# K loaded two groups to a transfer, its columns read in interleaved order, and wo's first 18 rows in one transfer

## The chip, the cores and the metric

The kernel runs on one core of a Trainium2 chip. The metric is the device time of one execution in microseconds (us). The kernel before took 100.55 us, the median of three runs (100.34 to 100.57).

The engines are named as in the profile: PE multiplies matrices (PEld loads its stationary operand), DVE and ACT work elementwise and reduce, POOL sets constants, and SP issues the DMA transfers. The engines run side by side and wait for each other on semaphores.

## The reference

The computation is one decoding step, for a single row x of 1024 values: attention with a sliding window beside a perceptron, both added to x.

```python
W = min(4096, max(256, Sk // 4))                  # 4096 of 65536 tokens
q = (xn @ wq).reshape(B, Sq, 32, 128)             # 32 query heads, xn = layernorm(x)
k = repeat(k_cache[:, :, Sk - W:, :], 8, axis=1)  # 4 groups of K and V, 8 heads each
v = repeat(v_cache[:, :, Sk - W:, :], 8, axis=1)
p = softmax(einsum("bhqd,bhkd->bhqk", q, k) * 128 ** -0.5)
A = einsum("bhqk,bhkd->bhqd", p, v).reshape(B, Sq, 4096) @ wo
Bm = gelu(layernorm(xn) @ w1 + b1) @ w2 + b2      # 1024 -> 3584 -> 1024
out = x + A + Bm
```

The parts that are read from the chip's memory, in bf16: K and V windows 4.19 MB each, wq 8.39 MB, wo 8.39 MB, w1 and w2 7.34 MB each. The profile counts 39.86 MB read.

## The kernel before

With one row of x each weight is used once. The row is the stationary operand and the weights stream through PE as the moving operand, 512 columns to a matmul. The transfers have an order written out by hand on SP's queue, and PE's program is in the same order:

1. SP issues K in four transfers (line 211), one for each of the four groups, then wq in two halves, then w1 in two halves.
2. DVE computes both layer norms, and then transposes K group by group into the tile KT (line 261), in blocks of 32 x 32. It waits for one K transfer before each of the four transposes.
3. When the last transpose is done, SP issues V into the tile KV that held K (line 264).
4. PE multiplies wq's rows (line 379, tile WA). The semaphore "q" releases SP to issue w2 into the same tile WA (line 269), and DVE to build the tile QBD of query columns.
5. PE multiplies the first half of w1 (`h_rows(0)`), then the scores (lines 409 to 414): 32 matmuls in two banks of 16, each with a stationary part of QBD and 512 columns of KT.
6. PE multiplies the second half of w1 (`h_rows(1)`) while DVE and ACT form the maximum, the exponentials and their transpose PT. The semaphore "h" releases SP to issue wo into the tile W1 (line 271).
7. PE forms the product of PT and V (line 454), then w2's rows (line 464) and then wo's rows (lines 479 to 492). wo's rows come in chunks of 10, 8, 6, 4, 2 and 1; a set of eight small transfers into the tile LOW, issued between the second and third chunk, holds the remaining row, split over two halves of the partitions. PE waits for each chunk's semaphore before its rows, and for ACT's two copies (line 357) before the last seven rows, whose results are packed differently (`tail_row`).
8. ACT and DVE copy the result, and SP stores it (line 365).

K's layout matters here. Before, partition p of KV holds, for each group, the 32 tokens 32p to 32p+31 with 128 values each. DVE's transpose exchanges partition and column inside each block of 32 x 32, so in KT the 32 tokens that lay in 32 partitions lie side by side. V stays in the layout that K had, and so the scores' columns have to come out in the order (i, q): i the token within a partition, q the partition within its block of 32.

W1 is read by `h_cols` (line 386) with four neighbouring columns at a time and a step of 28 columns (56 bytes). DVE has reductions whose input is read with a step: line 246 with 16 bytes, line 256 with 128 bytes, line 348 with 512 bytes. Line 297 reduces a contiguous row.

Of the kernel before, what the change touches and what calls it, by code (L numbers as in the profile page):

```python
# [9 lines left out]
D = 1024  # L10
F = 3584
HQ = 32
HKV = 4
DH = 128
REP = HQ // HKV
SK = 65536
W = 4096
# [3 lines left out]
W1_CHUNKS = [4, 4]  # L21
WQ_CHUNKS = [4, 4]
W2_CHUNKS = [16, 12]
WO_CHUNKS = [10, 8, 6, 4, 2, 1]
WO_HEAD = 4
WO_LOW = 18
XW = 136
QG = 520
# [22 lines left out]
def bass_parallel_sum__sliding_block_cached__mixer_channel_mlp__decode_kernel(  # L51
# [17 lines left out]
    pe, dve, act, pool, sp = nc.tensor, nc.vector, nc.scalar, nc.gpsimd, nc.sync  # L69

    def sems(name, n):
        return [nc.alloc_semaphore(f"{name}{i}") for i in range(n)]
# [2 lines left out]
    s_low = nc.alloc_semaphore("s_low")  # L75
    s_w1 = sems("s_w1", len(W1_CHUNKS))
    s_wq = sems("s_wq", len(WQ_CHUNKS))
    s_k = sems("s_k", HKV)
    s_wo = sems("s_wo", len(WO_CHUNKS))
    s_w2 = sems("s_w2", len(W2_CHUNKS))  # L80

# [6 lines left out]
    def sb(name, shape, d):  # L88
        return nc.alloc_sbuf_tensor(name, shape, d)
# [40 lines left out]
    KV = sb("KV", [128, 16384], bf16)  # L130
    KT = sb("KT", [128, 16384], bf16)
    W1 = sb("W1", [128, KC * F], bf16)
# [6 lines left out]
    def bank(n, rows=128, first=0):  # L139
        return PS[first:first + rows, n * 512:(n + 1) * 512]  # L140
# [4 lines left out]
    wo_p = A_wo.rearrange("(p j) n -> p j n", j=32)  # L145
# [4 lines left out]
    def load_chunks(dst, src, chunks, width, semaphores, c0=0):  # L150
        for j, n in enumerate(chunks):
            sp.dma_start(  # L152
                dst[:, c0 * width:(c0 + n) * width].rearrange("p (c n) -> p c n", c=n),
                src[:, c0:c0 + n, :],
            ).then_inc(semaphores[j], 16)
            c0 += n
# [51 lines left out]
    POOL.mark(pool.memset(PT[:, 1024:1024 + 96], 0.0))  # L208
    C["consts"] = POOL.cnt

    for g in range(HKV):
        sp.dma_start(  # L212
            KV[:, g * 4096:(g + 1) * 4096],
            A_k_cache[0, g, SK - W:SK, :].rearrange("(p i) d -> p (i d)", p=128)).then_inc(s_k[g], 16)
    load_chunks(WA, wq_p, WQ_CHUNKS, NQ, s_wq)
    load_chunks(W1, w1_p, W1_CHUNKS, F, s_w1)

# [39 lines left out]
        out=B32[:, :], in_=identf[:, :].rearrange("p (q r) -> p r q", q=4), axis=AX.X, op=ALU.add))  # L257

    for i in range(HKV):
        dve.wait_ge(s_k[i], 16)  # L260
        C["kt"] = DVE.mark(dve.transpose(KT[:, i * 4096:(i + 1) * 4096], KV[:, i * 4096:(i + 1) * 4096]))  # L261

    V = KV[:, :]
# [5 lines left out]
    sp.wait_ge(done["q"], 1)  # L269
    load_chunks(W2, w2_p, W2_CHUNKS, D, s_w2)  # L270
    sp.wait_ge(done["h"], 1)
    load_chunks(W1, wo_p, WO_CHUNKS[:2], D, s_wo)
    low_source = A_wo.rearrange("(u p j) n -> p u j n", u=2, j=32)[:, :, WO_MAIN, :]
    for first in (0, 1, 2, 3, 32, 33, 34, 35):
        sp.dma_start(  # L275
            LOW[first:first + 29:4, :].rearrange("p (u n) -> p u n", u=2),
            low_source[first:first + 29:4]).then_inc(s_low, 16)
    load_chunks(W1, wo_p, WO_CHUNKS[2:WO_HEAD], D, s_wo[2:], WO_LOW)
    load_chunks(WA, wo_p, WO_CHUNKS[WO_HEAD:], D, s_wo[WO_HEAD:], FC)

    dve.wait_ge(done["q"], 1)
# [123 lines left out]

    h_rows(0)
    pe.wait_ge(DVE.sem, C["d_QBD"])
    K5 = KT[:, :].rearrange("p (g i j k) -> p g i j k", g=HKV, i=32, j=4)
    for b in range(2):
        for n in range(16):  # L410
            g, j = n // 4, n % 4
            last = pe.matmul(bank(3 + b), lhsT=QBD[:, g * 512 + j * 128:g * 512 + j * 128 + 128],  # L412
                             rhs=K5[:, g, 16 * b:16 * b + 16, j, :], start=(n == 0), stop=(n == 15))
        last.then_inc(done["sc" if b else "sc0"], 1)
    def acc(a):
        return bank(7, 32, 32 * a)
# [35 lines left out]
    with pe.Fori(0, 4) as i:  # L452
        for u in range(8):
            pe.matmul(bank(1), lhsT=PT[:, bass.ds(i * 256 + u * 32, 128)], rhs=V4[:, :, bass.ds(i * 8 + u, 1), :],  # L454
                      start=False, stop=False, skip_group_check=True)
# [16 lines left out]
    for j in range(4):  # L472
        last = pe.matmul(PS[:, 2 * 512:2 * 512 + 32], lhsT=E4[:, j * 128:(j + 1) * 128],
                         rhs=ON[:, j * 32:(j + 1) * 32], start=(j == 0), stop=(j == 3))
# [3 lines left out]
    c0 = 0  # L478
    for j, n in enumerate(WO_CHUNKS):
        if c0 == WO_LOW:  # L480
# [6 lines left out]
        for c in range(c0, c0 + n):  # L487
            rhs = (W1 if c < FC else WA)[:, c * D:(c + 1) * D]
# [35 lines left out]
```

## Time and profile before

| What | Value |
|---|---|
| Median of three runs | 100.55 us |
| The profiled execution | 100.35 us |
| Its span, first to last instruction | 99.1 us |
| PE busy | 70.5 us (71%) |
| DVE busy | 37.5 us (38%) |
| DMA, mean over the span | 402 GB/s, 3286 packets |
| Scores (line 412), 32 matmuls | 7.1 us busy, first start 48.49 us |
| K transposes (line 261), 4 | 17.4 us busy, first start 17.18 us |
| K issues on SP | 0.80 to 3.00 us |

How to read it: the page cuts the span in 40 slices and gives the busy share of each in tenths. A group line names the line of the kernel, engine, operation, tiles and count, then busy time and mean ns of one, and then the idle time in front with what ended it. PE's matmuls overlap, so the distance between two starts, and not the duration of one, tells what a matmul costs in a stream. A timeline line begins with its start and its time in us. "DMA to landing" is the time from an issue to the last byte's arrival, and it includes the time in the queue.

### The profile page before, as it was taken

The numbers are of one execution on the slowest core, as the hardware profiler recorded it, in microseconds if no ns is written. First come the engines' busy times: TensorE is split into PE (matmuls) and PEld (weight loads), VectorE is DVE, ScalarE is ACT, GpSimd is POOL, SyncE is SP. The second block draws the span as 40 slices with busy tenths as digits, with TensorE's granted clock in tenths as the row PEclk, the third lists the DMA queues.
The fourth block names the chain that finished last, engine by engine and source line by source line (L and its number), as shares of the span: only waits on it lengthen the run. The fifth ranks groups of instructions, "written<-read, shape, count | busy, mean of one in ns | idle before, by whom it ended". The sixth has DMA issues, their size and how long they took to land.

```text
span 99.1 us, 1197 instructions
## 1 busy us (share of the span) xinstructions
PE 70.5 (71%) x341; PEld 28.4 (29%) x341; DVE 37.5 (38%) x56; ACT 5.7 (6%) x11; POOL 6.5 (7%) x26
## 2 busy tenths in 40 slices
PE   0021000305999999999999999799999999979532
PEld 0000000002334433334444344233335445422210
DVE  0007998999999900091002543440024010000001
ACT  0500004200000000000000040000000000000021
POOL 6990000000000000000000000000000000000000
PEclk9999999999999999999999999999999999999996
DMA  2999999999999889889799999998999999999960
GB/s 26 397 426 418 430 436 436 489 476 463 450 423 397 370 382 544 370 382 544 301 423 420 423 522 423 423 423 370 476 476 422 388 397 427 423 402 440 397 256 4
DMA packets 3286, 39.89 MB, mean 402 GB/s; under 512 B 594, under 2 KB 596, under 8 KB 980
## 3 DMA queue, kind: packets, MB, share of 16 engines
q1 hardware_dynamic: 3076, 39.85, 95.0%
q10 hardware_dynamic: 208, 0.01, 0.1%
q8 instruction: 1, 0.02, 0.1%
q14 instruction: 1, 0.01, 0.0%
HBM read 39.86 MB, written 0.00 MB: 402 GB/s over the span
## 4 chain that ended last, share of the span: by engine, by line
DMA 46%; PE 40%; SPq 10%; issue 2%; DVE 0%
PE PS L379 31%; DMA WA<-in_A_wo_dram 26%; DMA WA<-in_A_wq_dram 20%; PE PS L412 7%; SPq L275 6%; SPq L152 2%; SPq L212 2%; PE PS L383 1%; PE PS L436 1%; DVE Pb L363 0%; PE PS L430 0%
## 5 line engine op out<-in xcount | busy, mean ns | idle before, releaser
L379 PE MATMUL PS<-WA,XZ 128*128 x64 | 17.9, 433 | 5.6 <-DMA WA<-in_A_wq_dram 5.2
L261 DVE STREAM_TRANSPOSE KT<-KV 128x4096 bf16<-128x4096 bf16 x4 | 17.4, 4409 | 0.0
L379 PE MATMUL PS<-W,YZ 128*128 x56 | 13.0, 381 | 0.0
L464 PE MATMUL PS<-WA,GT 128*64 x56 | 12.5, 380 | 0.0
L379 PEld LDWEIGHTS PS<-WA,XZ 128*128 x64 | 6.9, 108 | 17.0 <-issue 13.2
L383 PE MATMUL PS<-XBRP,HOT 1*128 1x512 bf16 x6 | 2.5, 454 | 9.5 <-DVE XZ L253 9.5
L454 PE MATMUL PS<-KV,PT 128*128 x32 | 8.5, 378 | 0.7 <-issue 0.7
L464 PEld LDWEIGHTS PS<-WA,GT 128*64 x56 | 6.0, 110 | 5.8 <-issue 1.2
L379 PEld LDWEIGHTS PS<-W,YZ 128*128 x56 | 5.2, 96 | 7.5 <-issue 2.5
L412 PE MATMUL PS<-KT,QBD 128*128 128x512 bf16 x32 | 7.1, 379 | 0.0
L424 PE MATMUL PS<-W,OT 128*32 128x512 bf16 x48 | 5.7, 380 | 1.8 <-DMA W<-in_A_wo_dram 1.8
L363 DVE CAST Pb<-PS 64x256 bf16<-64x256 f32 x1 | 0.4, 417 | 16.1 <-PE PS L430 16.1
L373 PE MATMUL PS<-XBRP,onesb 1*128 1x512 bf16 x2 | 1.0, 605 | 6.7 <-DMA XBRP<-in_B_b_dram 6.7
L297 DVE TENSOR_REDUCE MX<-PS 128x1 f32<-128x512 f32 x2 | 1.4, 692 | 10.0 <-PE PS L412 10.0
L454 PEld LDWEIGHTS PS<-KV,PT 128*128 x32 | 3.1, 96 | 6.1 <-issue 2.7
L223 DVE BATCH_NORM_STATS2 BN<-PS 128x6 f32<-128x512 f32 x2 | 1.3, 688 | 7.7 <-PE PS L373 7.7
L412 PEld LDWEIGHTS PS<-KT,QBD 128*128 128x128 bf16 x32 | 3.1, 98 | 3.7 <-issue 0.2
L383 PEld LDWEIGHTS PS<-XBRP,HOT 1*128 1x128 bf16 x6 | 0.5, 94 | 11.5 <-issue 11.5
L342 DVE SCALAR_TENSOR_TENSOR QBD<-PS,REC,GMASK 32x512 f32<-32x512 f32 x1 | 0.7, 739 | 7.9 <-PE PS L383 7.9
L424 PEld LDWEIGHTS PS<-W,OT 128*32 128x32 bf16 x48 | 2.1, 97 | 5.3 <-DMA W<-in_A_wo_dram 2.8
L282 DVE CAST Pb<-PS 128x512 bf16<-128x512 f32 x1 | 0.7, 692 | 7.4 <-PE PS L383 7.4
L308 ACT ACTIVATE Pb<-PS,NMB 128x1024 bf16<-128x1024 f32 x1 | 1.1, 1114 | 40.1 <-DVE NMB L305 40.1
(79 smaller groups left out, 33.4 us busy)
## 6 DMA issues: line engine op xcount, KB each, us to landing
WA<-in_A_wq_dram SPq DMA_DIRECT2D x2, 4096.0 KB, 24.4
W<-in_B_w_dram SPq DMA_DIRECT2D x2, 3584.0 KB, 41.0
KV<-in_A_k_cache_dram SPq DMA_DIRECT2D x4, 1024.0 KB, 7.9
KV<-in_A_v_cache_dram SPq DMA_DIRECT2D x4, 1024.0 KB, 20.6
WA<-in_B_w_dram SPq DMA_DIRECT2D x1, 4096.0 KB, 27.2
WA<-in_B_w_dram SPq DMA_DIRECT2D x1, 3072.0 KB, 34.2
W<-in_A_wo_dram SPq DMA_DIRECT2D x1, 2560.0 KB, 21.4
W<-in_A_wo_dram SPq DMA_DIRECT2D x1, 2048.0 KB, 25.9
```

The costliest lines, as they stand in the source:

```text
L152: sp.dma_start(dst[:, c0 * width:(c0 + n) * width].rearrange("p (c n) -> p c n", c=n), src[:, c0:c0 + n, :],).then_inc(semaphores[j], 16)
L212: sp.dma_start(KV[:, g * 4096:(g + 1) * 4096], A_k_cache[0, g, SK - W:SK, :].rearrange("(p i) d -> p (i d)", p=128)).then_inc(s_k[g], 16)
L223: DVE.mark(dve.bn_stats(out=BN[:, 12 * n + 6 * i:12 * n + 6 * i + 6], in_=src[:, 512 * i:512 * i + 512]))
L261: C["kt"] = DVE.mark(dve.transpose(KT[:, i * 4096:(i + 1) * 4096], KV[:, i * 4096:(i + 1) * 4096]))
L275: sp.dma_start(LOW[first:first + 29:4, :].rearrange("p (u n) -> p u n", u=2), low_source[first:first + 29:4]).then_inc(s_low, 16)
L297: DVE.mark(dve.tensor_reduce(out=MX2[:, b:b + 1], in_=S[:, 512 * b:512 * b + 512], axis=AX.X, op=ALU.max))
L379: pe.matmul(bank(n), lhsT=vec[:, bass.ds(t + width * k, 128)], rhs=rhs_at(k, t), start=False, stop=False, skip_group_check=True)
L383: return pe.matmul(bank(n), lhsT=HOT[:, 8:136], rhs=XB[0:1, 0:8, :], start=start, stop=not start, skip_group_check=True)
L412: last = pe.matmul(bank(3 + b), lhsT=QBD[:, g * 512 + j * 128:g * 512 + j * 128 + 128], rhs=K5[:, g, 16 * b:16 * b + 16, j, :], start=(n = ...
L424: ins = pe.matmul(acc(a), lhsT=window(vec, c, a), rhs=rhs[:, a * 512:(a + 1) * 512], start=False, stop=stop, tile_position=(0, 32 * a), sk ...
L454: pe.matmul(bank(1), lhsT=PT[:, bass.ds(i * 256 + u * 32, 128)], rhs=V4[:, :, bass.ds(i * 8 + u, 1), :], start=False, stop=False, skip_gro ...
L464: pe.matmul(bank(7, 64), lhsT=GT[:, bass.ds(i * (4 * STEP) + (LEAD + STEP * (c0 + u) - ROW - a), 64)], rhs=W2[:, bass.ds(i * 4 * D + ((c0 ...
```

## The change

K comes in two transfers of two groups each. The 64 tokens 64m to 64m+63 of a group, 16 KB, go to one partition, and the two groups of a transfer alternate: partition 2m has the first group and partition 2m+1 the second. DVE transposes the same four blocks of 4096 columns; a block now holds 32 of the 64 tokens of both groups. In KT, the columns of one group are every second one of a run of 32 (index m, a step of 4 bytes), and the two halves of its 64 tokens (index e) lie 4096 columns or 8 KB apart. To keep the order (i, q) that PT and V need, with q = 2m + e, the scores' matmuls read i, then m, then e innermost. Each of the 512 columns of a matmul is read once, and there are still 32 matmuls with the same stationary operands. DVE waits twice, not four times.

wo's first two chunks, 10 and 8 rows, become one transfer of 18 rows (36 KB per partition) with one semaphore. The numbers that split the list of chunks shift by one.

```diff
-WO_CHUNKS = [10, 8, 6, 4, 2, 1]
-WO_HEAD = 4
+WO_CHUNKS = [18, 6, 4, 2, 1]
+WO_HEAD = 3
...
-    s_k = sems("s_k", HKV)
+    s_k = sems("s_k", 2)
...
-    for g in range(HKV):
+    for c in range(2):
         sp.dma_start(
-            KV[:, g * 4096:(g + 1) * 4096],
-            A_k_cache[0, g, SK - W:SK, :].rearrange("(p i) d -> p (i d)", p=128)).then_inc(s_k[g], 16)
+            KV[:, c * 8192:(c + 1) * 8192],
+            A_k_cache[0, 2 * c:2 * c + 2, SK - W:SK, :].rearrange("g (m i) d -> m g (i d)", m=64)).then_inc(s_k[c], 16)
...
     for i in range(HKV):
-        dve.wait_ge(s_k[i], 16)
+        if i % 2 == 0:
+            dve.wait_ge(s_k[i // 2], 16)
         C["kt"] = DVE.mark(dve.transpose(KT[:, i * 4096:(i + 1) * 4096], KV[:, i * 4096:(i + 1) * 4096]))
...
-    load_chunks(W1, wo_p, WO_CHUNKS[:2], D, s_wo)
+    load_chunks(W1, wo_p, WO_CHUNKS[:1], D, s_wo)
...
-    load_chunks(W1, wo_p, WO_CHUNKS[2:WO_HEAD], D, s_wo[2:], WO_LOW)
+    load_chunks(W1, wo_p, WO_CHUNKS[1:WO_HEAD], D, s_wo[1:], WO_LOW)
...
-    K5 = KT[:, :].rearrange("p (g i j k) -> p g i j k", g=HKV, i=32, j=4)
+    K7 = KT[:, :].rearrange("p (c e i j m a) -> p c a j i m e", c=2, e=2, i=32, j=4, m=16)
     for b in range(2):
         for n in range(16):
             g, j = n // 4, n % 4
             last = pe.matmul(bank(3 + b), lhsT=QBD[:, g * 512 + j * 128:g * 512 + j * 128 + 128],
-                             rhs=K5[:, g, 16 * b:16 * b + 16, j, :], start=(n == 0), stop=(n == 15))
+                             rhs=K7[:, g // 2, g % 2, j, 16 * b:16 * b + 16], start=(n == 0), stop=(n == 15))
```

## The prediction

> **What bounds the kernel now.** I read the chain of waits first, then the landing times in the views of the K, V and weight loads, then the timeline from the scores to the end.
>
> ```profile
> PE   0021000305999999999999999799999999979532
> DMA  2999999999999889889799999998999999999960
> ...
> PE PS L379 31%; DMA WA<-in_A_wo_dram 26%; DMA WA<-in_A_wq_dram 20%; PE PS L412 7%; SPq L275 6%; SPq L152 2%; SPq L212 2%; PE PS L383 1%; PE PS L436 1%; DVE Pb L363 0%; PE PS L430 0%
> ...
> DMA to landing us min/median/max: 4.8/7.9/11.0
> ...
> 23.39 18.30 PE L379 MATMUL PS<-WA,XZ 128*128 x64 [5.19 <-DMA WA<-in_A_wq_dram]
> 48.49 7.07 PE L412 MATMUL PS<-KT,QBD 128*128 128x512 bf16 x32
> 56.04 6.31 PE L379 MATMUL PS<-W,YZ 128*128 x28
> 86.12 2.33 PE L424 MATMUL PS<-W,OT 128*32 128x512 bf16 x20
> 89.01 1.91 PE L424 MATMUL PS<-W,OT 128*32 128x512 bf16 x16 [0.56 <-DMA W<-in_A_wo_dram]
> 92.70 1.47 PE L424 MATMUL PS<-W,OT 128*32 128x512 bf16 x12 [1.25 <-DMA W<-in_A_wo_dram]
> 97.08 0.29 PE L430 MATMUL PS<-WA,OT 128*32 128x256 bf16 x4 [0.24 <-DMA WA<-in_A_wo_dram]
> ...
> L297 DVE TENSOR_REDUCE MX<-PS 128x1 f32<-128x512 f32 x2 | 1.4, 692 | 10.0 <-PE PS L412 10.0
> L246 DVE TENSOR_REDUCE XNT<-PT 128x8 f32<-128x1024 bf16 x1 | 1.9, 1944 | 0.0
> L348 DVE TENSOR_REDUCE ON<-QBD 32x128 bf16<-32x512 f32 x1 | 1.0, 1028 | 0.0
> L256 DVE TENSOR_REDUCE B<-identf 128x32 f32<-128x128 f32 x1 | 0.4, 359 | 0.0
> ```
>
> Two resources run almost level. The DMA row is full from the second slice to the last but one, so the transfers stand in one queue and the end is set by the total of their packets: K's four parts land at 5.6, 8.2, 10.7 and 13.2 us, then wq's halves at 22.9 and 32.6, and the last row of wo at 97.03. The chain names PE for the middle and wo's DMA for the end; the "issue to landing" pieces in it are mostly time in that queue. PE works from 23.39 without a real wait until it meets wo, and its first waits there (0.56, 1.25, 1.02, 0.62 and 0.24 us) show how little it is ahead. So a few us more on PE become the end.
>
> How much may PE be late? From the first wo matmul at 86.12, laid end to end: 26 pairs of matmuls at 217 ns a pair with the last one's 0.38 is 5.81; two changes of chunk cost 0.1 each (a start distance of 309 against 215 ns at LOW), 0.2; ACT's two copies with a wake-up on both sides, 0.83; the last 7 rows at 112 ns with the last one's 0.28, 0.95. That ends at 93.91. From PE's last end (97.37) to the span's end is 1.73. PE alone would finish the span at 95.64, DMA does at 99.1. The slack is 3.5 us.
>
> **The change, part by part.** The sum is made against the profiled execution: span 99.1 and 1.25 around it, 100.35 us. The median of the three timed runs is 100.55, so I add 0.2 at the end.
>
> K's transfers: four of 128 rows of 8 KB become two of 128 rows of 16 KB. In the trace's packet records an 8 KB packet takes a median of 312 ns, a 16 KB one 613, a 32 KB one 1215. Per DMA engine 32 x 312 = 9.98 us becomes 16 x 613 = 9.81: 0.18 saved, which moves wq's landing, PE's start and every later landing. Completions cost nothing visible: eight packets of 312 are 2.50 us, and the parts land 2.50 to 2.55 apart. Two SP issues go (0.41 and 0.42 us); the queue is filled well ahead of the engines, so they save nothing.
>
> DVE loses two of four waits and the first transpose needs 2 MB, not 1 MB. It starts at 17.18, after the layer norm, 4 us after all of K has landed: nothing. The four transposes (4.40 us each) are the same, so V's issue at 34.62 stays.
>
> wo's first 18 rows in one transfer: per engine 8 x (764 + 613 ns) for 20 KB and 16 KB packets becomes 8 packets of 36 KB. With 37.6 ns per further KB (1215 minus 613, over 16) one takes 1365: 0.10 saved. One SP issue (0.33 to 0.44 us) goes, so the eight LOW issues and the rest come earlier, and all still wait behind W2 in the queue. PE now may not start at 86.12 but only when the 18th row has landed, at 88.97 less 0.28. From 88.7 its remaining 7.79 us end at 96.5, before the last landing (96.75). The cover is thin, 0.3 us, and holds.
>
> Together the transfers give 0.28 us, if they run at the paces seen. The bounds: none (any loss is a rival below), to 0.5 if K reaches wq's pace (the parts span 10.1 us, a half of wq, also 4 MB, 9.7).
>
> The scores: 32 matmuls start 216 ns apart and fill 48.65 to 55.56, and no wait lies inside. Their columns are now read as (i, m, e): the innermost index has two steps, 8 KB apart, the next moves 4 bytes. So no two columns read after each other are neighbours. Before, runs of 32 columns (64 bytes) were. No PE row shows this. The nearest rows:
> - Below: L379 reads W1 in runs of 4 columns (8 bytes) with a step of 56 bytes, 219 ns inside its loop against 216 for L412. A column alone could be free, and a gain is excluded since 216 is the best distance of any 512-column matmul here.
> - Above: if those runs of 4 are the shortest that hide the fetch, a fetch takes up to 219/4 columns, 1.71 ns each of 128 runs, and 512 single columns take 876 ns.
> - DVE's strided reductions: 1.94 us for 1024, 1.03 for 512, 0.36 for 128 elements (steps of 16, 512 and 128 bytes) lie on a line of 1.755 ns an element plus 0.135; the contiguous L297 has 0.692 for 512, 1.09 ns. As a time per fetch that gives 899 ns on PE; as a ratio (1.61) 348 ns.
> - PE's own two paces: the first wq matmuls, from 23.4 to 29, start 427 ns apart, 0.83 ns per column; afterwards 216. If the warm pace is two neighbouring columns in that step, columns without a neighbour fall back to 427.
>
> I take 427, the row of the same engine between the ends: 32 x 211 = 6.75 us. [...]
>
> What the 6.75 us meet: two maxima, exp and PT's transpose come later by it and so does W1's second half, and h ends near 69.3 in place of 62.67. wo's issue waits for that; W2's last landing is at 76.6, so DMA has 7 us of queue left and is not starved. W2 has landed before PE gets to it. So the first wo matmul starts at 86.12 - 0.18 + 6.75 = 92.69, when 24 rows have landed, PE runs through in 7.79 to 100.48, and the span ends 1.73 later at 102.21. Time: 103.46, on the median's scale **103.7 us**, 3.1% slower. In general the span is 95.46 + X for X us more in the scores, and 98.8 if that is less.
>
> **Rivals.**
> 1. Single columns are cheap. Up to X = 3.4 us (321 ns a matmul) all is hidden and the transfers decide: 100.35 - 0.28 + 0.2 = **100.3**, between 100.0 and 100.6. For it: 219 ns in runs of 4, and DMA ending last. It stops being slower by 0.3% below X = 3.9 us (339 ns). Against it: three DVE reductions with three strides, all at 1.755 ns.
> 2. A fetch per column at its full price, 876 to 899 ns: X = 21.1 to 21.8, span 116.6 to 117.3, time **118.0 to 118.7**. For it: the two figures, from two engines, agree within 3%. DMA then idles some 7 us before wo, still ahead of PE. Against it: it takes PE's port to be no faster than DVE's.
> 3. DVE's ratio, or something else between: 348 ns is X = 4.2, span 99.7, **101.1**; a triple 648 ns would be X = 13.8, 110.7.
> 4. K's rows slow the transfer: neighbouring partitions now read from two heads 16 MB apart. wo's first transfer shows the size of a disturbance: 2.6 MB between 76.56 and 84.05, 7.5 us against 6.1 for its eight packets; the same 1.22 on K's 10 us is 2.2, and a halved pace is 10 us more before PE's start. With cheap columns that gives **102.5 to 110.5**, with 427 ns 105.9 to 113.7. Nothing in the profile shows such an alternation; against it, wq's partitions are 64 KB apart, K's 8 KB, and wq's half still takes 9.7 us. [...]
>
> **How the numbers follow.** Forecast (near 427 ns) 0.37; rival 1 0.25; rival 2 0.22; rival 3 0.10; rival 4 0.06. The range must hold the forecast and rivals 1 and 2, since each holds more than 0.2: 100.0 to 118.7. The forecast's own range is 102.5 to 105 (400 to 460 ns, and the transfers' 0 to 0.5). Changes within 0.3%, 0.3 us, are about what timing this kernel can't tell from none. Rival 1 straddles that line: 0.17 of it faster (a hidden price and transfers that gain at least what I count), 0.07 the same, 0.01 slower (X between 3.9 us and where I would no longer call it cheap); all the others are slower, 0.75.
>
> **What the profile after would show.** The start distance in L412's group is the test: 216, about 430, or about 880 ns. With 427 the group takes 13.7 us, h's edge matmul comes near 69, and wo's matmuls start at 92.7 with no DMA wait among them; the chain is then PE to the end. With 216, PE waits for the 18 rows until 88.7, and the last wait is on wo's last row, 0.3 earlier. K should land at about 8.0 and 13.0; a second landing after 15 is rival 4, and after 17.2 it would hold up DVE's transposes. The prediction is wrong if PE reads alternating single columns at full pace, if a fetch costs more than 0.83 ns, or if K's transfers change pace.

## The result, and the profile after

The changed kernel took 107.98 us (median of five runs, 107.95 to 109.71) beside 100.56 for the kernel before. The ratio is 1.072, with a 95% interval of 1.067 to 1.078. The prediction had the sign and the path (slower scores make PE late at the end), but 103.7 us: 7.4 us were lost where 3.1 were forecast. The time lies within its wide range of 100.0 to 118.7.

Some executions of a kernel take 1.3 to 1.8 us more than its others, so the lines below come from a second profile of the changed kernel, at 107.95 us, and differences of less than 1 us are read from landing times rather than from medians.

The chain of waits after the change, in order of time (start, us, what), names PE from wq's landing to the end, apart from four steps of 0.35 to 0.69 us on DVE and ACT. These are its pieces around the scores and at the end.

```profile
42.51 6.65 PE PS L380 x28
49.16 17.13 PE PS L413 x32
66.28 0.55 PE PS L437 x2
66.83 6.24 PE PS L380 x28
...
97.15 5.95 PE PS L425 x52
```

The scores' 32 matmuls, 6.91 us before, now fill 17.13: 535 ns from start to start and not 216. W1's half in front of them and the one behind, 6.65 and 6.24 us, are what they were. The last line is the prediction's picture of the end: all 52 matmuls of wo's first 24 rows in one piece, with no wait for DMA among them. The timeline shows the same, and the start of PE:

```profile
23.90 9.00 PE L380 MATMUL PS<-WA,XZ 128*128 x32 [4.77 <-DMA WA<-in_A_wq_dram]
...
48.99 17.29 PE L413 MATMUL PS<-KT,QBD 128*128 128x512 bf16 x32
...
97.08 4.06 PE L425 MATMUL PS<-W,OT 128*32 128x512 bf16 x36
101.07 0.61 PE L425 MATMUL PS<-KT,OT 64*32 64x512 bf16 x4
101.61 1.47 PE L425 MATMUL PS<-W,OT 128*32 128x512 bf16 x12
```

wo's first matmul starts at 97.08, 10.96 us later than before. Of that 10.22 are the scores, 0.50 is there already when q is done (42.12 against 41.62), and 0.24 comes in the PV loop. The span grew by only 7.6 us, to 106.7: the other 3.36 us are the slack that PE had against the transfers. The 0.50 is the second surprise: PE starts on wq at 23.90 and not at 23.39. K's transfers were to gain 0.18 us and lost instead.

### The profile page after: what moved, and what is told of

It reads as the page before. It is cut to its first block, busy times and chain, and to the rows that moved or that the text cites. A ratio compares the mean times of both kernels' runs of the same rounds, so it can differ in the third digit from the quotient of the medians.

```text
span 108.5 us, 1194 instructions
## 1 busy us (share of the span) xinstructions
PE 81.9 (75%) x341; PEld 29.0 (27%) x341; DVE 37.5 (35%) x56; ACT 5.7 (5%) x11; POOL 6.5 (6%) x26
## 4 chain that ended last, share of the span: by engine, by line
PE 74%; DMA 19%; issue 2%; SPq 1%; DVE 1%; ACT 1%
PE PS L380 30%; DMA WA<-in_A_wq_dram 19%; PE PS L413 16%; PE PS L465 11%; PE PS L455 8%; PE PS L425 5%; SPq L212 1%; PE PS L384 1%; PE PS L431 1%; ACT PS L358 1%; DVE H L315 1%; PE PS L437 1%; DVE Pb L364 0%; PE PS L450 0%; PE PS L474 0%
## 5 line engine op out<-in xcount | busy, mean ns | idle before, releaser
L262 DVE STREAM_TRANSPOSE KT<-KV 128x4096 bf16<-128x4096 bf16 x4 | 17.4, 4410 | 0.0
L413 PE MATMUL PS<-KT,QBD 128*128 128x512 bf16 x32 | 17.3, 698 | 0.0
L380 PE MATMUL PS<-W,YZ 128*128 x56 | 14.7, 416 | 0.0
```

The source lines that it names most:

```text
L380: pe.matmul(bank(n), lhsT=vec[:, bass.ds(t + width * k, 128)], rhs=rhs_at(k, t), start=False, stop=False, skip_group_check=True)
```

## The experiments: reading the scores' columns

The theory after the result: KT is read in lines of 16 bytes (eight bf16 columns; which runs show the 16 is said under the price of a line), and a change of line from one column to the next costs a time of its own. A fresh line is one that the matmul has not read yet. The rivals: the jump of 8 KB to and fro costs; or columns are fast only where they are direct neighbours. All distances below are from start to start in the middle of the 32 matmuls, as the traces have them.

**Which part of the change it is.** The reading order alone, on the kernel before:

```diff
-    K5 = KT[:, :].rearrange("p (g i j k) -> p g i j k", g=HKV, i=32, j=4)
+    K7 = KT[:, :].rearrange("p (c e i j m a) -> p c a j i m e", c=2, e=2, i=32, j=4, m=16)
...
-                             rhs=K5[:, g, 16 * b:16 * b + 16, j, :], start=(n == 0), stop=(n == 15))
+                             rhs=K7[:, g // 2, g % 2, j, 16 * b:16 * b + 16], start=(n == 0), stop=(n == 15))
```

> Only the reading order (i, m, e) of the scores; K in four transfers and wo in six as before. The columns meet the wrong tokens, so this is not the same attention. Theory: the reading alone makes the 535 ns, 10.2 us in the scores, and the slack of 3.5 us takes off what it can: 107.2 us. Rival: the 535 ns come with the new layout in KT, as DVE writes it, and with the old one the distance is 216 to 430 ns and the time below 104 us.

Measured: 535 ns and 107.61 us, ratio 1.072 (1.061 to 1.083). The reading alone makes 7.0 of the 7.4 us, and the layout as DVE writes it has no part in the 535 ns.

K's part alone, with wo in six chunks:

```diff
-WO_CHUNKS = [18, 6, 4, 2, 1]
-WO_HEAD = 3
+WO_CHUNKS = [10, 8, 6, 4, 2, 1]
+WO_HEAD = 4
```

> K's two transfers and the new reading order, wo in six chunks as before. Theory: PE is late by 10 us when it meets wo, so how wo is cut does not matter: 108.0 us, as with both parts. Rival: the wo transfer holds part of the loss, and this kernel is at least 0.5 us faster than the changed one.

Measured: 108.24 us, ratio 1.075 (1.067 to 1.082), 535 ns. How wo is cut makes no difference that shows once PE is late.

The changed kernel twice more, without an edit:

> The changed kernel once more. Theory: each column of the scores that lies on another 16-byte line of KT than the column before it takes 535/512 = 1.045 ns, so the 32 matmuls start 535 ns apart and fill 17.1 us, 10.2 us more than before; PE then runs without a wait from wq to the end and the time is 108.0 us. Rival: the 535 ns belong to one disturbed execution, in which the clock was granted at half for 3.4 us after the scores, and an undisturbed one shows about 430 ns and 104.5 us.

> The changed kernel, to see where 108.0 and 109.8 us differ. Theory: in the longer executions the clock is granted at half for 3.41 us right after the scores, and W1's second half takes 7.9 in place of 6.2 us; in one of 108.0 us the clock stays at full and all else is equal.

Both showed 535 ns in the scores. The first had 109.83 us (ratio 1.086, 1.076 to 1.095), the second 107.95. The windows over W1's second half give the difference; the first fence is the execution of 109.71 us, the second the one of 107.95 (columns: window and length; busy us and count of PE, PEld, DVE, ACT, POOL; granted clock; DMA share; GB/s):

```profile
66.87:74.80 7.93, 7.93 (x30) 3.03 (x29) 2.85 (x11) 1.21 (x2) 0.00 (x0) 0.78 0.98 420
```

```profile
66.40:72.80 6.40, 6.40 (x30) 2.62 (x28) 3.21 (x11) 1.21 (x2) 0.00 (x0) 1.00 1.00 429
```

The clock was granted at half for 3.41 us directly behind the slow matmuls, and W1's half took 7.90 us, not 6.24. So the rival (535 ns belong to one disturbed execution) fell, and the 1.7 us are a further loss in some executions. That the slow matmuls bring it on is not shown: the kernel before has executions some 1.3 us longer too, and none of those was traced.

**Steps of two are free, and so are columns that are no neighbours.** In the changed kernel, e outside m:

```diff
-    K7 = KT[:, :].rearrange("p (c e i j m a) -> p c a j i m e", c=2, e=2, i=32, j=4, m=16)
+    K7 = KT[:, :].rearrange("p (c e i j m a) -> p c a j i e m", c=2, e=2, i=32, j=4, m=16)
```

> The changed kernel with e outside m: columns in steps of two (4 bytes), 16 in a row, then 8 KB away for 16 more. The scores' columns then stand in another order than V's rows, so this is not the same attention. Line theory: four columns after each other share a 16-byte line, as in W1's runs of four, so 219 ns and 100.9 us. Neighbour theory: PE is fast only for columns that are direct neighbours in memory, so 430 to 535 ns and 104.5 to 108 us.

Measured: 216 to 217 ns; 100.88 to 102.37 us, as for the same loads with runs of 32 below. And in the kernel before, in the order 0, 4, 1, 5, 2, 6, 3, 7 within each 16 bytes:

```diff
+    K8 = KT[:, :].rearrange("p (x l h m) -> p x l m h", x=32, h=2, m=4)
...
+                             rhs=K8[:, 8 * g + 2 * j + b], start=(n == 0), stop=(n == 15))
```

> The kernel before, with the scores' columns in the order 0, 4, 1, 5, 2, 6, 3, 7 within each 16 bytes: no two columns after each other are neighbours, and the line changes every eight columns. Not the same attention, since the columns are not the right tokens. Line theory: 216 to 220 ns, 100.5 us. Neighbour theory: 430 ns or more, 103.5 us or more.

Measured: 216 ns, 100.43 us in one execution. The neighbour theory fell with these two: neither reads two neighbours after each other, and both are at full pace. The "steps of two" cost nothing; e inside m does.

**The price of a line.** Three readings on the kernel before; steps of 16 bytes at one place (every column on a fresh line), steps of 8 bytes (two columns to a line), and steps of 16 bytes at two places 8 KB apart in turn:

```diff
+                             rhs=KT[:, g * 4096 + 2 * j + b:(g + 1) * 4096:8], start=(n == 0), stop=(n == 15))
```

```diff
+    K8 = KT[:, :].rearrange("p (x n s) -> p x n s", x=8, s=4)
...
+                             rhs=K8[:, n // 2, :, 2 * (n % 2) + b], start=(n == 0), stop=(n == 15))
```

```diff
+    K8 = KT[:, :].rearrange("p (c e x n s) -> p c x n e s", c=2, e=2, x=2, s=8)
...
+                             rhs=K8[:, g // 2, g % 2, :, :, 2 * j + b], start=(n == 0), stop=(n == 15))
```

> The kernel before, with the scores' columns in steps of 16 bytes through one group: each column on the next line, no far jump. The columns are not the right tokens, so this is not the same attention. Line theory: 535 ns, 107.2 us. Distance theory (the alternation between two places 8 KB apart is what costs): 216 to 220 ns and 100.5 us. If a line that is left and taken up again matters, something between.

> The kernel before, with the scores' columns in steps of 8 bytes: two columns on each line, then the next line. Not the same attention, since the columns are not the right tokens. Time per fresh line (1.758 ns, whatever is read of it): 256 x 1.758 = 450 ns, X = 7.5 us, 104.8 us. [...]

> The kernel before, with the scores' columns read in turn from two places 8 KB apart as in the changed kernel, but in steps of 16 bytes at each place, so that no line is met twice within a matmul. Not the same attention, since the columns are not the right tokens. Revisit theory: a fresh line costs 1.758 ns (900/512, steps of 16 bytes at one place), and the 1.045 ns of the changed kernel come from lines that are met four times in turn: 900 ns and about 122 us. Alternation theory: going to and fro between two places is what makes a change of line cheaper: 535 ns and 107.5 us.

The group of the scores in the three pages, in that order (busy us, mean ns of one matmul):

```profile
L411 PE MATMUL PS<-KT,QBD 128*128 128x512 bf16 x32 | 29.0, 1077 | 0.0
```

```profile
L412 PE MATMUL PS<-KT,QBD 128*128 128x512 bf16 x32 | 14.6, 631 | 0.0
```

```profile
L412 PE MATMUL PS<-KT,QBD 128*128 128x512 bf16 x32 | 31.0, 1144 | 0.0
```

From start to start these are 900, 452 and 963 ns. 900/512 is 1.758 ns a line and 452/256 is 1.766: the same time per fresh line, whether one column or two are read of it. With four columns to a line it is at most 1.69 to 1.72 (216 to 220 ns over 128 lines, as in the steps of two above and in W1's runs of four), where 1.758 would make 225. DVE's three strided reductions are close to it (1.74 and 1.79 ns an element from one row to the next). Between two places it is 1.88.

That the line has 16 bytes follows from these distances. On lines of 8 bytes, steps of 16 and of 8 bytes would both put every column on a line of its own and cost the same, and on lines of 32 bytes W1's runs of 8 bytes, 56 bytes apart, would take as long as the steps of 8 bytes, not 219 ns. Nor is it the bytes passed over that cost: W1's matmuls pass over 7 KB, the steps of 8 bytes over 4 KB.

In the first and third kernel the clock was granted at half for most of the scores and at full in their first matmuls; the distance did not change with it. In these windows of the first (columns as above), the scores start 900 ns apart in the first two lines, and W1's matmuls 427 ns apart in the third and 219 in the fourth:

```profile
48.60:53.00 4.40, 4.40 (x6) 0.56 (x5) 0.00 (x0) 0.00 (x0) 0.00 (x0) 1.00 0.95 400
53.00:77.00 24.00, 24.00 (x28) 3.27 (x26) 0.69 (x1) 0.00 (x0) 0.00 (x0) 0.51 0.95 407
78.50:83.00 4.50, 4.50 (x12) 1.57 (x12) 2.44 (x9) 1.21 (x2) 0.00 (x0) 0.50 0.00 0
84.50:87.50 3.00, 3.00 (x15) 1.16 (x12) 0.00 (x0) 0.00 (x0) 0.00 (x0) 1.00 0.00 0
```

The times of the three kernels were 122.2 us (ratio 1.213, 1.202 to 1.224), 104.9 (one execution) and 123.8 (ratio 1.229, 1.217 to 1.240). The line theory's 535 ns for the first was wrong, and the distance theory's 216 too; the alternation theory's 535 for the third fell as well, so going to and fro is no cheaper by itself.

Pairs of neighbours in turn from two places:

```diff
+    K8 = KT[:, :].rearrange("p (c e x n m) -> p c x n e m", c=2, e=2, x=16, m=2)
...
+                             rhs=K8[:, g // 2, 8 * (g % 2) + 2 * j + b], start=(n == 0), stop=(n == 15))
```

> The kernel before, with pairs of neighbouring columns (4 bytes) read in turn from two places 8 KB apart. Not the same attention, since the columns are not the right tokens. Line theory: one line per 1.045 ns and two columns on each, 256 x 1.045 = 268 ns; X = 1.7 us, which is hidden: 100.5 us. Distance theory: a fixed price of (535 - 216)/512 = 0.62 ns for a jump, so 216 + 256 x 0.62 = 375 ns, X = 5.1 us, 102.1 us. Neighbour theory: 216 to 220 ns.

Measured: 271 ns (268 was the line theory's), 100.52 us, ratio 1.0005 (0.996 to 1.005): the 1.8 us more in the scores are hidden. Here, as in the changed kernel, each line is met four times, in turn with another: 271/256 is 1.06 ns a change, 535/512 is 1.045. Fresh lines in turn cost 1.88, so a change between lines that are met four times is cheaper. How the cost divides between the first meeting and the others is not shown: if the first cost 1.88 and the three others x, x would be 0.77 to 0.78 ns, and the two columns of a pair alone take 0.84 ns at 216 ns for 512, so the costs do not simply add up. No run here showed a return by itself.

**Two ways out.** The order could be made on the other side, in PSUM, with the cheap reading (on the kernel with K's part alone):

```diff
-            last = pe.matmul(bank(3 + b), lhsT=QBD[:, g * 512 + j * 128:g * 512 + j * 128 + 128],
+            last = pe.matmul(bank(3 + b).rearrange("p (i m e) -> p i e m", i=16, e=2), lhsT=QBD[:, g * 512 + j * 128:g * 512 + j * 128 + 128],
```

> K in two transfers, wo in six as before; the scores read steps of two with e outside m (217 ns measured), and the order that V needs is made on the other side, by writing the columns to PSUM with a step of two. The whole computation is kept. If PSUM takes a step of two at full pace: 217 ns and 100.9 us, the late start of K being all that is left. If the step costs there what it saves here: 430 ns or more and 104 us or more.

Measured: 429 ns, 104.83 us, ratio 1.040 (1.033 to 1.048). With a step of two (8 bytes) in what PE writes to PSUM the matmuls start 429 and not 217 ns apart, at a granted clock of 1.00 over the whole execution, so this is not the pace of a halved clock. Or DVE writes the two halves side by side:

```diff
-        C["kt"] = DVE.mark(dve.transpose(KT[:, i * 4096:(i + 1) * 4096], KV[:, i * 4096:(i + 1) * 4096]))
+        C["kt"] = DVE.mark(dve.transpose(
+            KT[:, (i // 2) * 8192:(i // 2 + 1) * 8192].rearrange("p (n e) -> p n e", e=2)[:, :, i % 2], KV[:, i * 4096:(i + 1) * 4096]))
...
-    K7 = KT[:, :].rearrange("p (c e i j m a) -> p c a j i m e", c=2, e=2, i=32, j=4, m=16)
+    K7 = KT[:, :].rearrange("p (c i j m a e) -> p c a j i m e", c=2, e=2, i=32, j=4, m=16)
```

> K in two transfers of 16 KB rows, wo in six; DVE's transposes write the two halves (e) of a group's tokens side by side, with a step of 4 bytes, so that the scores read (i, m, e) as two neighbours and a step of 8 bytes: four columns to a line. The whole computation is kept. Time per fresh line (128 x 1.758 = 225 ns, hidden or nearly): 217 to 225 ns in the scores. If DVE's step costs nothing (4.40 us each): 100.9 us. If it makes the transposes a half longer (6.6 us each, ending near 44.5): still 100.9, V's issue is hidden by the queue until 49; if it doubles them, V comes late and 103 us or more.

Its groups of the transposes and the scores:

```profile
L262 DVE STREAM_TRANSPOSE KT<-KV 128x4096 bf16<-128x4096 bf16 x4 | 18.5, 4707 | 0.0
...
L414 PE MATMUL PS<-KT,QBD 128*128 128x512 bf16 x32 | 7.2, 380 | 0.0
```

The scores run at 220 ns again, with four columns to a line, and the transposes take 18.5 us, not 17.4, which the queue of transfers hides. 101.1 us, ratio 1.003 (0.999 to 1.007): the whole computation with 16 KB rows, but not faster than the kernel before. None of the kernels tried here beats that one.

## The experiments: the slack and the transfers

**The slack.** In the changed kernel, 16 of the 32 matmuls in runs of 32 columns:

```diff
-                             rhs=K7[:, g // 2, g % 2, j, 16 * b:16 * b + 16], start=(n == 0), stop=(n == 15))
+                             rhs=K7[:, g // 2, g % 2, j, 16 * b:16 * b + 16] if n < 8 else K5[:, g, 16 * b:16 * b + 16, j, :], start=(n == 0), stop=(n == 15))
```

> The changed kernel with 16 of the 32 score matmuls (groups 0 and 1) in the new order and 16 in runs of 32 columns as before. The second kind meets the wrong tokens, so this is not the same attention. It tests the slack: the scores grow by 16 x 319 ns = 5.1 us. Prediction's sum (PE may be 3.5 us late, beyond that every us shows), from the 100.9 us of the two loads with cheap reading: 102.5 us. Rival, PE's lateness shows in full from the start: 106.0 us.

Measured: 103.0 us, ratio 1.022 (1.015 to 1.029), 2.1 us above the 100.9 of the loads alone. The scores grow by the 5.1 us expected, but PE is 5.45 us later by W2's last rows (86.85 and not 81.40), so 3.4 us are hidden, as in the changed kernel, where the prediction said 3.5. That PE's lateness shows in full is ruled out.

**wo in one piece**, alone:

```diff
-WO_CHUNKS = [10, 8, 6, 4, 2, 1]
-WO_HEAD = 4
+WO_CHUNKS = [18, 6, 4, 2, 1]
+WO_HEAD = 3
```

> Only wo's first 18 rows in one transfer; K and the scores as before. Theory: packets of 36 KB save 0.10 us in the queue and PE still starts early enough, so 100.45 us, no difference that can be measured. Rival: the single landing starts PE 2.6 us later (88.9 in place of 86.1) and its remaining 7.8 us end after wo's last landing: 100.8 us or more.

The end of its timeline:

```profile
89.12 4.06 PE L424 MATMUL PS<-W,OT 128*32 128x512 bf16 x36 [2.80 <-DMA W<-in_A_wo_dram]
...
97.11 0.29 PE L430 MATMUL PS<-WA,OT 128*32 128x256 bf16 x4 [0.23 <-DMA WA<-in_A_wo_dram]
```

PE waits 2.80 us for the 18 rows and still arrives 0.23 us ahead of wo's last row: the thin cover holds. From wq's first landing to wo's last are 74.06 us, before 74.15. That is the 0.1 that was predicted, but the kernels here with wo in six have 74.07 to 74.36, so it can't be told from scatter. The shortest time is 100.40 against 100.41, but the median is 101.62 against 100.55, the ratio 1.007 (1.002 to 1.011). The three kernels with wo's 18 rows in one transfer and the scores at full pace (this one, both loads below, steps of two above) have medians 1.1 to 1.2 us above their shortest times; with wo in six (the kernel before, the pairs, the three of 100.7 to 101.1 us) it is 0.1 to 0.3. So the single transfer seems to cost something in most executions. The traces, taken of short ones, don't show what, and the cause stays open.

**Both loads with the reading of before** (the changed kernel with the old K5 and its reading):

> Both transfers as changed, but the scores read runs of 32 columns as before. The scores' columns then meet the wrong tokens, so this is not the same attention; the work on every engine is as large as before. Prediction's term: the transfers alone gain 0.28 us, 100.3 us. Rival, from the changed kernel's trace, in which wq's first half lands at 23.5 and not 22.9: K's two transfers begin late by 0.6 us and cost that much more than the packets save, 100.9 to 101.2 us.

Measured: 100.85 us at the shortest, median 101.95, ratio 1.011 (1.005 to 1.018). wq's first half lands at 23.47 and not 22.88, wo's last row at 97.60 and not 97.03. The rival is right: the transfers lose 0.4 to 0.6 us. In the packet records the 16 KB packets take a median of 611 ns, as predicted, and summed over a DMA engine K's packets take 10.20 us where they took 10.34, so 0.14 is saved. But the first one starts at 2.46 us and not 1.82, and 0.64 less 0.14 is about the 0.6 by which wq lands late. SP's first issue takes 0.67 us:

```profile
L212 SPq DMA_DIRECT2D KV<-in_A_k_cache_dram x2: 673/727/781, 0.8 to 1.5; - x2
```

Three kernels looked for the cause. K in two transfers with rows of 8 KB (the first edit), with rows of 16 KB from a single place (the second, both on the kernel before), and x's issue held back, on the kernel with the order in PSUM (the third):

```diff
+            KV[:, c * 8192:(c + 1) * 8192].rearrange("p (g n) -> p g n", g=2),
+            A_k_cache[0, 2 * c:2 * c + 2, SK - W:SK, :].rearrange("g (p i) d -> p g (i d)", p=128)).then_inc(s_k[c], 16)
```

```diff
+            KV[:, c * 8192:(c + 1) * 8192],
+            A_k_cache[0, 2 * c, SK - 2 * W:SK, :].rearrange("(p i) d -> p (i d)", p=128)).then_inc(s_k[c], 16)
```

```diff
+    act.wait_ge(POOL.sem, 3)
     row_load(XB[0:1], A_x.rearrange("b s n -> (b s) n"), s_x)
```

> The kernel before with K in two transfers of two groups, but in rows of 8 KB, so that KT and the scores' reading are as before. The whole computation is kept. If two groups in one transfer make the first issue long (0.67 in place of 0.41 us) and the first packet late (2.46 in place of 1.82): the same here, wq's first half near 23.5, 101.0 us. If it is the 16 KB rows: 1.82, 22.9 and 100.5 us.

> The kernel before with K in two transfers of 16 KB rows, each from one contiguous place of 2 MB (the last 8192 tokens of groups 0 and 2), so that the transfer has a single group as its source. It reads other tokens than the reference's, so this is not the same attention. If two groups in one transfer make it late: issue 0.41, first packet 1.82, wq's first half at 22.7, 100.3 us. If it is the 16 KB rows: first packet near 2.46, 100.9 us.

> As the one before, and ACT waits for POOL's third constant (about 1.65 us) before it issues x, so that K's first issue, which now takes 0.67 us and not 0.41, is the first to finish. Theory: the first K packet starts at 2.46 us and not 1.82 since SP's issue ends after ACT's (1.47 against 1.40 us) and x's packets are set up ahead of K's; here it starts at about 2.1, wq's first half lands at 23.1, and with a cheap order in PSUM the time is 100.5 us. Rival: the start is late because a source with two groups takes longer to set up: 2.46 us and 100.9 us as before.

| Kernel | K's first issue, us | First packet, us | First 16 packets, mean us | wq's first half, us |
|---|---|---|---|---|
| before | 0.41 | 1.82 | 0.71 | 22.88 |
| both loads | 0.67 | 2.46 | 0.98 | 23.47 |
| two groups, 8 KB | 0.46 | 1.91 | 0.68 | 23.22 |
| one source, 16 KB | 0.41 | 1.82 | 1.15 | 23.51 |
| two groups, 16 KB, x held back | 0.67 | 2.25 | 1.03 | 23.55 |

The first three columns say that the late start needs both, two groups and rows of 16 KB. With both loads, all 16 DMA engines are late together: half of them have finished wq's first half by 23.30 us, before by 22.74, and the last is 0.30 us behind the first, before 0.31. The kernel with one source lands as late for another reason. It starts on time, and half of its engines are done by 22.84, but the slowest is 1.2 us behind the fastest (22.30 to 23.51), and its first packets take up to 1.82 us. Holding x back moved the start by 0.2 us; wq landed 0.15 us earlier than in the kernel that it is an edit of (23.55 and not 23.70), less than the kernels with 16 KB rows differ among themselves (23.39 to 23.83). So neither of its two theories is settled. wq's first half lands at 23.2 us or later in all kernels with K in two transfers, and between 22.9 and 23.1 in those with four. The times were 100.77 us (ratio 1.005, 1.0005 to 1.010), 100.74 (1.002, 0.997 to 1.007) and 104.57 (1.038, 1.032 to 1.043, with the 429 ns in it). Why the start is late with two groups in rows of 16 KB, and why the engines drift apart with one source, stays open.

## Why the prediction was wrong, and where right

- **The scores' term was mis-sized**: 32 x 211 = 6.75 us were put in, 10.22 were measured. The step that failed is the choice of 427 ns, "the row of the same engine between the ends". That row has the pace that the runs show at half clock: W1's matmuls start 427 ns apart where the clock was granted at 0.50 and 219 at 1.00 (the four windows above), and in the kernel before the trace's record of a full clock begins at 29.21 us, where wq's 427 ns end. It says nothing of the order of columns, and the scores' 900 ns did not follow the clock at all. The price is that of a line. The nearer rows were there, and were read as an end of the range: W1's runs of four (1.71 ns a line) and DVE's 1.755 ns (its three rows give 1.74 to 1.79). A fresh line did cost 1.76 (900 ns over 512 lines, 452 over 256). What neither shows, and the prediction did not see in the new order, is that each line is met four times, in turn with another, and that such a change costs 1.045 ns. Rival 2 had the right price of a fresh line, but took every column for one. That the time fell between the forecast and rival 2 is not to the range's credit: no term of it stood for lines met again.
- **K's transfers**: 0.18 us were to be gained, by packets of 613 for two of 312 ns. The packets did run at 611, and 0.14 of the 0.18 is there in an engine's sum; the term left out the start, which came 0.64 us later, and PE began 0.51 us later. That "the queue is filled well ahead of the engines" does not hold for the first transfer.
- **wo in one transfer**: 0.10 us predicted; the 0.09 found in the queue is within the scatter, and the median rose by 1.1 us, which no term of the prediction stood for. The cover of 0.3 us for PE's late start was 0.23.
- **DVE and V**: the transposes took 4.40 us each, as said. They start at 18.1 and not 17.18, since PE's first matmul waits for x and b2's row, and the latter lands at 7.48 and not 6.57; V's issue moves to 35.54, which the queue hides.
- **The slack and the sum**: with 10.22 in place of 6.75, PE's start 0.68 later than the sum had it, and 0.24 in the PV loop that it did not foresee, its span of 102.21 becomes 106.6; 106.7 was measured. The slack of 3.5 us was 3.4. PE's end from the first wo matmul took 7.9 us where 7.79 were laid end to end.
- **Rivals**: cheap single columns (1) fell for this order, though not for steps of two. K's rows 16 MB apart (4) did not slow the packets (611 ns). No run shows the halved pace that the upper ends of that rival stand on: in the profile after, K's two parts landed at 8.83 and 13.78 us, 0.8 us later than forecast. (The upper end of its first span should be 110.3, 100.3 and 10 us, not 110.5.)

## What to carry to other kernels

A matmul's moving operand was priced here by lines of 16 bytes: about 1.76 ns for each fresh line when one or two columns of it were read, and nothing above the 216 to 220 ns for 512 columns when four bf16 columns of each line were read one after the other (three were not tried). Their order within the line and a step of two were free (216, and 216 to 217 ns), an innermost index that leaves the line was not (535 ns), and an order that is needed is best made where an engine has time, here in DVE's write (18.5 us of transposes in place of 17.4, hidden). A pace of an engine is to be held against the granted clock before it is taken for the price of an access. An access pattern is costed by writing out its first eight columns with their lines, before looking for a row with a like step. And a saving per packet in the first transfer of a kernel is to be read from a trace: its start is not the steady queue (here 0.14 us saved and 0.64 us lost).

## What the runs showed of the hardware that was not expected

- PE took 1.758 to 1.766 ns per fresh line and DVE 1.74 to 1.79 ns per strided element, and on PE it did not change when the granted clock was halved (900 ns a matmul at 1.00 and at 0.51).
- Lines met in turn cost less when they were met again: 1.045 and 1.06 ns a change with four meetings, 1.88 with one.
- A step of two in PE's writes to PSUM: 429 ns, not 216.
- The clock was halved for 3.41 us directly after 17 us of slow matmuls in an execution of 109.71 us, though PE was counted busy all the time.
- The first 16 packets of K took 0.68 and 0.71 us each on average with 8 KB and 0.98 to 1.15 with 16 KB (the table above), where the median of all packets of these sizes is 0.31 and 0.61.
